# Windowed attention and an ELU layer on one core: the mask instructions of GpSimd placed ahead of two value loads

## The chip, the cores and the metric

The kernel runs on one core of a Trainium2 chip. The metric is the device time of one execution in microseconds (us), of which the median of several runs is taken. The engines are TensorE (PE in the profile; its weight loads are PEld), VectorE (DVE), ScalarE (ACT), GpSimd (POOL) and SyncE (SP). Each has an instruction stream of its own and executes it in order; semaphores tie the streams together. SP, ACT and GpSimd also issue DMA transfers.

## The reference, cut to what matters

The inputs are q, k and v of shape 8 x 8 x 576 x 64 (batch, heads, sequence, head size), and the two weights w_in (512 x 2048) and w_out (2048 x 512), all float32. Attention sees 32 positions to either side; its heads, side by side, are the 4608 x 512 input of a two-layer network with an ELU between the layers:

```python
scores = scale * np.matmul(q, k.transpose(0, 1, 3, 2))
mask = np.abs(pos[:, None] - pos[None, :]) <= 32
scores = np.where(mask, scores, -1000000000.0)
scores = scores - np.max(scores, axis=-1, keepdims=True)
attn = np.exp(scores)
attn = attn / (np.sum(attn, axis=-1, keepdims=True) + 1e-09)
x = np.matmul(attn, v)            # then heads side by side: 4608 x 512
h = x @ w_in
g = np.where(h > 0.0, h, np.exp(np.minimum(h, 0.0)) - 1.0)
out = g @ w_out
```

## The kernel before, in words

Queries are taken in blocks of 64, nine to a batch element, and two blocks make a pair: 36 pairs of 128 tokens. A block looks at 128 keys. For one pair `scores` (line 385) multiplies keys and queries of all eight heads into PSUM, `exponential` (396) takes the exponential on ScalarE into `pu`, `mask` (405) multiplies it on DVE with a band of zeros and ones into `pm`, `pv` (417) multiplies with the values, and `normalize` (426, 429) divides by the sum, which a column of ones in the values gives. Pairs 0 to 3 are treated otherwise: `band` (365) adds a large negative number outside the window to their scores beforehand, from a tile `far`, so that they need no `mask`. The first pair that reads the tile `masks` is pair 4.

The values of a batch element lie in SBUF twice, once from an even block's first key (`V_e`, five pieces) and once shifted by 64 keys (`V_o`, four pieces). For the first element the four pieces of `V_o` are loaded by `load_v_odd` (line 159) and most of `V_e` is copied from them by DVE in `rotate_back` (166). Pair 2 reads `V_o` piece 2 and what was copied from it, pair 3 reads piece 3.

Two pairs make a tile of 256 tokens for the network, 18 tiles in all. A step takes 256 of the 2048 hidden columns: `mm1` multiplies with `w_in` (755), ScalarE takes the exponential (764), DVE or ScalarE subtracts one (775, 773), DVE puts the ELU together (786), and `mm2` multiplies with `w_out` (806). That makes 144 steps; the attention of later pairs is set into them by a table of steps and places, written by hand. Nothing is reordered by a planner: each engine's stream is in the order in which the code calls.

Ahead of the steps stands a front, in straight code. GpSimd, which also converts from float32 to bfloat16 while it loads, issues in this order: `far` and the first fill of `masks` (246 to 257), two pieces of `V_o` with half a piece of `V_e` between them, two pieces `c` of k and q (`load_cast`, 146), the w_in of step 0, the pieces 2 and 3 of `V_o`, the w_in of step 1 in two quarters, the w_in of steps 2 and 3 as one, two parts of w_out (208), the last half piece of `V_e`, two small pieces of q and k, and one more part of w_out. Then come the masks, and after them, from line 547 on, the rest of the weights and the second batch element.

`make_masks` (263 to 278) has five `affine_select` instructions on GpSimd, each of which changes `masks` in place and puts a zero wherever a linear condition on partition and column fails: two on all five 64-column bands (lines 264 and 267), and three on a single band each (271 twice, 275). Beside them, SP and ACT load the first half of q and k at the start, and PE, DVE and ScalarE work through the front of pairs 0 to 3.

Of the kernel before, what the change touches and what calls it, by code (L numbers as in the profile page):

```python
# [21 lines left out]
def kernel(  # L22
# [115 lines left out]
    def load_cast(b, which, part):  # L138
        z, nj = part
        mj = nj if nj < 3 else HJ + 1  # L140
        t = cpool.tile([128, 2, mj * D], BF16, tag=f"c{which}{mj}",
                       name=f"c{which}")[:, :, 0:nj * D]
        qk_c[b, which, z] = t
        src = (q, k)[which][b, :, z:z + NC * nj, :].rearrange(
            "(g h) (c j) d -> c g h (j d)", h=2, j=nj)
        nc.gpsimd.dma_start(out=t, in_=src)
# [10 lines left out]
    def load_v_odd(b, m):  # L157
        lo = 128 * m + WIN
        nc.gpsimd.dma_start(  # L159
            out=V_o[b % 3][:, m, :, 0:D],  # L160
            in_=v[b, :, lo:lo + 128, :].rearrange("h p d -> p h d"))
# [35 lines left out]
    def load_w_in(c, z=0, nz=1):  # L197
        w = D_FF // 4 // nz
        c = c * nz + z
        nc.gpsimd.dma_start(  # L200
            out=w_in_sb[:, :, c * w:(c + 1) * w],
            in_=moe_w_in[:, c * w:(c + 1) * w].rearrange(
                "(o p) f -> p o f", p=128))

    def load_w_out(c, z=0, nz=1):
        n = NFO // 4 // nz
        c = c * nz + z
        nc.gpsimd.dma_start(
            out=w_out_sb[:, c * n:(c + 1) * n, :],
            in_=moe_w_out[c * n * 128:(c + 1) * n * 128, :].rearrange(  # L210
                "(o p) f -> p o f", p=128))
# [51 lines left out]
    def make_masks():  # L263
        nc.gpsimd.affine_select(
            out=masks, in_=masks, compare_op=ALU.is_ge, fill=0.0,
            base=0, pattern=[[0, 5], [-1, QB]], channel_multiplier=1)
        nc.gpsimd.affine_select(
            out=masks, in_=masks, compare_op=ALU.is_ge, fill=0.0,
            base=2 * WIN, pattern=[[0, 5], [1, QB]], channel_multiplier=-1)
        for mi in (0, 4):  # L270
            nc.gpsimd.affine_select(
                out=masks[:, mi, :], in_=masks[:, mi, :],
                compare_op=ALU.is_ge, fill=0.0, base=-WIN,
                pattern=[[0, QB]], channel_multiplier=1)
        nc.gpsimd.affine_select(
            out=masks[:, 3, :], in_=masks[:, 3, :], compare_op=ALU.is_ge,
            fill=0.0, base=128 - WIN - 1, pattern=[[0, QB]],
            channel_multiplier=-1)
# [209 lines left out]
    for which in (1, 0):  # L488
        load_cast(0, which, FRONT_B[which])
    load_w_in(0, 0, 2)  # L490
    for m in (2, 3):
        load_v_odd(0, m)
    for z in (2, 3):
# [5 lines left out]
    for which in range(2):  # L499
        load_cast(0, which, FRONT_C[which])  # L500
    load_w_out(1, 0, 2)
    make_masks()

    idle(10, "y1")
    BOTH = (nc.scalar, nc.vector)
# [401 lines left out]
```

## Time and profile before

| What | Value |
|---|---|
| Median of three runs | 301.42 us (300.98 to 301.87) |
| Profiled execution, its own time | 301.24 us |
| Its span in the profile | 299.5 us |
| PE busy | 294.3 us (98%) |
| DVE busy | 240.7 us (80%) |
| ACT busy | 168.9 us (56%) |
| POOL (GpSimd) busy | 56.4 us (19%) |
| GpSimd's DMA queue (q0) | 45552 packets, 10.03 MB, 43.5% of 16 engines' span |
| The four loads of `V_o`, issue to landing | 4.9 / 6.2 / 7.2 us (least, median, greatest) |
| The five mask instructions | 0.50, 0.47, 0.24, 0.24 and 0.24 us |

Times inside an execution count from the start of the span. The profile is of one execution; what lies around its span (1.74 us) belongs to the time but not to the view. A row of the view in order of time has the start, the duration, the engine, the line, the operation with what it writes and reads, and in brackets the idle time before it with what ended it. Where several instructions of a kind follow one another, one row holds them (x2, x3). A GpSimd row with an operation DMA_DIRECT2D is the issue of a transfer, the writing of its descriptors, and not the transfer itself.

### The profile page before, as it was taken

What the parts mean: (1) busy time and instruction counts of PE and PEld (TensorE: products, weight loads), DVE (VectorE), ACT (ScalarE), POOL (GpSimd) and SP (SyncE); (2) the same over time, 40 slices, a digit from 0 to 9 for tenths busy, and PEclk for the clock granted to TensorE, in tenths of its full rate; (3) what the DMA queues carried; (4) which work ended last, traced back from release to release, by engine and by line L of the source; (5) the groups of instructions that cost most, each with busy time, mean ns of one, the idle gap of its engine ahead of it and who ended that gap; (6) DMA issues with size and microseconds to landing.
All of it is one profiled execution on the core that took longest, in us unless ns stands there. A gap on an engine that the chain in (4) does not pass through costs nothing.

```text
span 299.5 us, 7747 instructions
## 1 busy us (share of the span) xinstructions
PE 294.3 (98%) x3132; PEld 198.7 (66%) x3132; DVE 240.7 (80%) x478; ACT 168.9 (56%) x256; POOL 56.4 (19%) x81
## 2 busy tenths in 40 slices
PE   7999999999999999999999999999999999999996
PEld 3576666676666666666666666666666666666764
DVE  7776787988788888888888789887988787876773
ACT  3883458698655567456745765467535353534342
POOL 8878604520005000410032002300000000000000
PEclk9999999999999999999999999999999999999999
DMA  9999999999968949999899989996921121111012
GB/s 191 173 198 203 189 252 412 355 141 258 205 159 203 239 121 263 231 278 140 161 256 302 192 211 249 311 154 136 272 52 72 35 72 38 70 37 70 2 70 71
DMA packets 94789, 52.74 MB, mean 176 GB/s; under 512 B 78242, under 2 KB 84642, under 8 KB 94754
## 3 DMA queue, kind: packets, MB, share of 16 engines
q1 hardware_dynamic: 47330, 35.68, 44.9%
q0 software_dynamic: 45552, 10.03, 43.5%
q10 hardware_dynamic: 1872, 6.55, 6.3%
q8 instruction: 24, 0.39, 0.6%
q14 instruction: 11, 0.09, 0.1%
HBM read 36.70 MB, written 15.34 MB: 174 GB/s over the span
## 4 chain that ended last, share of the span: by engine, by line
PE 91%; DVE 2%; DMA 2%; POOL 2%; ACT 1%; issue 1%; POOLq 0%; DVEq 0%
PE ps L755 41%; PE psY L806 40%; PE psS L417 4%; PE psS L385 3%; DMA c<-in_q_dram 2%; PE ptx L341 1%; PE psXT L439 1%; DVE m_sb L775 1%; ACT e_sb L764 1%; POOL Vo L159 1%; PE ptx L336 1%; DVE g_sb L786 0%; DVE y_sb L293 0%; ACT pu L396 0%; PE psS L365 0%
## 5 line engine op out<-in xcount | busy, mean ns | idle before, releaser
L764 ACT ACTIVATE e_sb<-ps 128x512 f32<-128x512 f32 (+1 forms) x145 | 86.1, 595 | 112.6 <-PE ps L755 105.7
L755 PE MATMUL ps<-xT,w_in_sb 128*128 128x256 bf16 (+1 forms) x1184 | 149.6, 270 | 0.0
L806 PE MATMUL psY<-w_out_sb,g_sb 128*128 128x512 bf16 (+2 forms) x592 | 147.2, 374 | 0.0
L755 PEld LDWEIGHTS <-w_in_sb 128*128 128x128 bf16 x1184 | 111.0, 98 | 36.6 <-DVE g_sb L786 0.5
L786 DVE SCALAR_TENSOR_TENSOR g_sb<-ps,m_sb 128x512 bf16<-128x512 f32 (+1 forms) x145 | 99.4, 687 | 13.2 <-DVE m_sb L775 0.5
L775 DVE TENSOR_SCALAR m_sb<-e_sb 128x512 bf16<-128x512 f32 (+1 forms) x142 | 61.2, 431 | 33.0 <-ACT e_sb L764 30.8
L806 PEld LDWEIGHTS <-g_sb 128*128 128x128 bf16 x592 | 55.8, 98 | 38.3
L152 POOL DMA_DIRECT2D Ve<-in_v_dram x37 | 32.1, 878 | 128.5 <-PE psS L417 79.5
L396 ACT ACTIVATE pu<-psS 128x1024 bf16<-128x1024 f32 x36 | 36.5, 1021 | 1.4 <-PE psS L385 1.4
L429 DVE TENSOR_TENSOR x_st<-psS,rc 128x512 bf16<-128x512 f32 x36 | 24.9, 692 | 1.2
L291 ACT CAST qkb<-f 128x768 bf16<-128x768 f32 (+2 forms) x29 | 25.1, 864 | 0.6 <-DMA f<-in_q_dram 0.5
L405 DVE TENSOR_TENSOR pm<-pu,masks 128x1024 bf16<-128x1024 bf16 x32 | 21.8, 682 | 0.5 <-ACT pu L396 0.5
L417 PEld LDWEIGHTS <-pm 128*64 128x64 bf16 x512 | 9.6, 110 | 7.3 <-DVE pm L405 6.9
L293 DVE COPY y_sb<-psY 128x512 f32<-128x512 f32 (+1 forms) x18 | 12.2, 676 | 1.4 <-PE psY L806 1.4
L385 PEld LDWEIGHTS <-kT 64*128 64x128 bf16 x560 | 9.4, 95 | 4.7 <-issue 4.0
L291 ACT COPY y_sb<-psY 128x512 f32<-128x512 f32 (+1 forms) x19 | 10.8, 567 | 2.8 <-PE psY L806 2.8
L385 PE MATMUL psS<-qT,kT 64*128 64x64 bf16 x560 | 11.9, 191 | 0.2
L417 PE MATMUL psS<-Ve,pm 128*64 128x65 bf16 x288 | 11.5, 196 | 0.1
L417 PE MATMUL psS<-Vo,pm 128*64 128x65 bf16 x224 | 10.3, 196 | 0.0
L176 DVE COPY Vo<-Ve 64x1040 bf16<-64x1040 bf16 (+2 forms) x22 | 9.1, 414 | 0.7
L291 ACT COPY kT<-ptx 128x512 bf16<-128x512 bf16 (+4 forms) x7 | 6.6, 963 | 2.8 <-PE ptx L336 2.3
L426 DVE RECIPROCAL rc<-psS 128x8 f32<-128x8 f32 x36 | 7.2, 199 | 0.6 <-PE psS L417 0.4
(58 smaller groups left out, 94.4 us busy)
## 6 DMA issues: line engine op xcount, KB each, us to landing
out_dram<-y_sb SPq DMA_DIRECT2D x35, 256.0 KB, 3.8
f<-in_q_dram SPq DMA_DIRECT2D x12, 576.0 KB, 6.9
f<-in_k_dram SPq DMA_DIRECT2D x12, 576.0 KB, 8.7
in_dram<-qkb ACTq DMA_DIRECT2D x10, 576.0 KB, 4.2
Ve<-in_v_dram POOLq DMA_DIRECT2D x21, 128.0 KB, 11.8
w_out_sb<-in_moe_w_out_dram POOLq DMA_DIRECT2D x8, 256.0 KB, 8.9
Ve<-in_v_dram POOLq DMA_DIRECT2D x14, 96.0 KB, 10.8
w_in_sb<-in_moe_w_in_dram POOLq DMA_DIRECT2D x5, 256.0 KB, 7.6
```

The costliest lines, as they stand in the source:

```text
L152: nc.gpsimd.dma_start(out=V_e[b % 3][p0:p1, m, :, 0:D], in_=v[b, :, lo + p0:lo + p1, :].rearrange("h p d -> p h d"))
L291: nc.scalar.copy(d_, s_)
L385: nc.tensor.matmul(psS[:, h % 2, hp * 128 + z * QB:hp * 128 + (z + 1) * QB], lhsT=keys, rhs=qT[b % 2][base:base + 64, hp, QB * qb:QB * (qb ...
L396: nc.scalar.activation(pu, _bap(psS, [psS.ap[0], [1, 1024]]), AX.Exp, scale=SCALE)
L405: nc.vector.tensor_mul(pm, pu, _bap(mm, [mm.ap[0], [0, H], [1, 2 * QB]]))
L417: nc.tensor.matmul(psS[QB * z:QB * (z + 1), par, hp * VD:(hp + 1) * VD], lhsT=pm[:, par * HP + hp, z * QB:(z + 1) * QB], rhs=vv[:, qb // 2 ...
L429: nc.vector.tensor_mul(x_st, _bap(psS, [psS.ap[0], [VD, HP], [512, 2], [1, D]]), _bap(rc, [rc.ap[0], [2, HP], [1, 2], [0, D]]))
L755: nc.tensor.matmul(o, lhsT=w_in_sb[:, do, fo * 128:(fo + 1) * 128], rhs=r, start=(do == 0), stop=(do == NDO - 1))
L764: nc.scalar.activation(e_sb, ps, AX.Exp)
L775: nc.vector.tensor_scalar(m_sb, e_sb, -1.0, None, ALU.add)
L786: nc.vector.scalar_tensor_tensor(g_t[kk][:, z * w:(z + 1) * w, :], ps, 0.0, m_t.pop((kk, z)), ALU.max, ALU.min)
L806: nc.tensor.matmul(sum_of(t, ts, c), lhsT=(g_t[n][:, j, :] if n >= BY_ROWS else g_t[n][:, j, ts * 128:(ts + 1) * 128]), rhs=w_out_sb[:, fi ...
```

## The change

The call of `make_masks` is moved up in the front: past the last part of w_out, two small pieces of q and k, half a piece of `V_e`, two parts of w_out, three loads of w_in and the two value pieces 2 and 3. It now stands right behind the w_in of step 0. No instruction is added, removed or altered, and the streams of the other engines keep their order.

```diff
     for which in (1, 0):
         load_cast(0, which, FRONT_B[which])
     load_w_in(0, 0, 2)
+    make_masks()
     for m in (2, 3):
         load_v_odd(0, m)
     for z in (2, 3):
@@
     for which in range(2):
         load_cast(0, which, FRONT_C[which])
     load_w_out(1, 0, 2)
-    make_masks()
 
     idle(10, "y1")
```

## The prediction

> **What bounds the kernel now.** I read the page's busy shares first: PE is busy for 294.3 us of the 299.5 us span, so a change counts only if it opens or closes a gap on PE. The chain of work that ended last then tells what releases PE in the stretch of the change:
>
> ```profile
> 3.58 0.59 POOL Ve L152
> 4.17 0.88 POOL Vo L159
> 5.05 0.66 POOL c L146
> 5.71 6.18 DMA c<-in_q_dram
> 11.89 0.04 issue
> 11.93 0.58 PE ptx L336 x14
> ```
>
> The reader is to see that GpSimd's issues set the end only up to 5.71 us, and that from 11.93 us on PE carries the chain, to 33.8 us without a break. The masks now run at 16.93 us; they are on no part of it. Next, GpSimd's instructions in order of time (start, duration, engine, line, what, idle time before and its releaser):
>
> ```profile
> 5.71 0.71 POOL L146 DMA_DIRECT2D c<-in_q_dram  x1
> 6.41 0.77 POOL L200 DMA_DIRECT2D w_in_sb<-in_moe_w_in_dram  x1
> 7.16 1.79 POOL L159 DMA_DIRECT2D Vo<-in_v_dram  x2
> 8.90 2.28 POOL L200 DMA_DIRECT2D w_in_sb<-in_moe_w_in_dram  x3
> 11.16 0.72 POOL L208 DMA_DIRECT2D w_out_sb<-in_moe_w_out_dram  x1
> 12.17 0.71 POOL L208 DMA_DIRECT2D w_out_sb<-in_moe_w_out_dram  x1 [0.29 <-DMA c<-in_q_dram]
> 13.49 0.60 POOL L152 DMA_DIRECT2D Ve<-in_v_dram  x1 [0.60 <-DMA w_in_sb<-in_moe_w_in_dram]
> 14.59 0.70 POOL L146 DMA_DIRECT2D c<-in_q_dram  x1 [0.51 <-DMA Vo<-in_v_dram]
> 15.53 0.71 POOL L146 DMA_DIRECT2D c<-in_k_dram  x1 [0.23 <-DMA Vo<-in_v_dram]
> 16.23 0.70 POOL L208 DMA_DIRECT2D w_out_sb<-in_moe_w_out_dram  x1
> 16.93 0.50 POOL L264 TENSOR_SCALAR_AFFINE_SELECT masks<-masks 128x320 bf16<-128x320 bf16 x1
> ...
> 18.61 0.77 POOL L200 DMA_DIRECT2D w_in_sb<-in_moe_w_in_dram  x1
> ```
>
> Counted from the first value load, the 13th issue waits for the 5th transfer (c of q), the 14th for the 6th (w_in), the 15th and 16th for the 7th and 8th (the values of pairs 2 and 3): GpSimd runs at most eight transfers ahead, and in this stretch it is the transfers that hold it up. Last, who needs those values, from DVE's and PE's weight loads in order of time:
>
> ```profile
> 14.33 0.61 DVE L166 COPY Ve<-Vo 64x520 bf16<-64x520 bf16 x2 [0.37 <-DMA Vo<-in_v_dram]
> ...
> 15.26 0.29 DVE L166 COPY Ve<-Vo 64x520 bf16<-64x520 bf16 x1 [0.32 <-DMA Vo<-in_v_dram]
> ```
>
> ```profile
> 15.19 0.20 PEld L417 LDWEIGHTS <-pu 128*64 128x64 bf16 x8 [0.21 <-ACT pu L396]
> ```
>
> Pair 2's values land at about 14.3 us, the copies end at 14.94 us, and PE starts that pair's value products at 15.19 us, having waited for ScalarE. So pair 2's landing has 0.25 us to spare; pair 3's (copy ends 15.55, products at 16.11) has 0.56 us.
>
> **What the Trainium skill says.** "DMA: Bandwidth & Descriptors", section "SWDGE vs HWDGE vs iDMA": GpSimd writes descriptors into rings, which the DMA engines drain; its subsection "Two DMAs through the same engine are not ordered" adds that within one queue of one engine descriptors start in order. So a transfer issued late is late only if its queue has run out of earlier ones. The trace agrees that there is a backlog: the first two value loads, with next to nothing before them on that queue, took 4.9 and 5.2 us from issue to landing, those of pairs 2 and 3 some 7.2. Same page, "Anatomy of one DMA — SWDGE (gpsimd) path": 2.0 us fixed plus bytes at 436 GB/s, an estimate of 2.3 us for the 128 KB here; the trace's 4.9 us beside the first q and k loads is more than twice that, and I use the trace's. "SBUF — State Buffer", section "Who interferes with whom": DVE instructions in a two-port mode and GpSimd block one another for a whole instruction, others with at most one SBUF input do not. The trace fits: DVE's PSUM copy of 128x512 at 18.12 us, under the mask instructions, took 0.42 us, as did the one at 13.54; the SBUF-sourced m_sb at 18.46 took 0.48 against a mean of 0.431.
>
> **The change part by part.** Nothing is added or removed. Five mask instructions (0.50 + 0.47 + two of 0.24 + 0.24) occupy GpSimd from 16.93 to 18.61 us: 1.68 us. They move to 7.16 us, past eleven transfers: two value loads, three of w_in, two of w_out, one of Ve, two of c, one of w_out. All are on GpSimd's queue; SP's queue is passed by nothing.
>
> *The two value loads.* Issues go from 7.16 and 8.03 us to 8.84 and 9.71. What hides this is the backlog. With an empty queue a load would take 4.9 to 5.2 us, so they would land by 14.0 and 14.9 us; the c's and the w_in ahead of them hold them until 14.3 and 15.25 anyway. Cost 0. The margin is 0.3 us in the queue plus 0.25 us on PE: a stall begins only if a value load with nothing before it needs more than 14.56 - 8.84 = 5.7 us. With the backlog gone, the cost would be 1.68 - 0.25 = 1.43 us. I take 0, and keep 0 to 1.43.
>
> *The three w_in loads.* The quarters of step 1 are issued at about 10.6 and 11.3 us; at 5.2 us each they would land by 15.8 and 16.5, and PE first needs them at 16.49 and 17.19. The 512 KB piece goes from some 10.43 to 12.1 us. It took the page's 8.6 us, landing at 19.03, behind the backlog. Empty, I estimate 5.2 us plus 384 KB more at the page's 200 GB/s, 1.9 us: landing at 19.2. Its first product is at about 20.0 us (the 48 products end at 21.77; the last sixteen, of 0.109 us each, are those that need it). Cost 0, at worst what the values cost, not in addition.
>
> *The other six.* The first w_out goes out at 12.84, the second at 13.56 without its 0.29 us wait, Ve at 14.28 without its 0.60. The next two still wait for the values, landing as before, so they go out at about 14.9 and 15.6 against 14.59 and 15.53, and the third w_out at 16.3. Of 1.68 us only about 0.1 is left there: the waits of 0.29 + 0.60 + 0.51 + 0.23 = 1.63 us absorb the rest. Their users come after 21 us. Cost 0.
>
> *What is gained behind.* The w_in load of 18.61 us can be issued at about 17.0. But the queue is full: the page's DMA row stands at 9 through this stretch, and the c issued at 20.85 waits 0.77 us for a w_out to land. An earlier place in a full queue brings no earlier landing. At most, the DMA wait that PE's weight loads show later (0.42 us at 30.36) would go: I take 0 and keep -0.4 to 0.
>
> *DVE and the masks' new neighbours.* Between 7.16 and 8.84 us DVE ends a cast from SBUF at 7.29, then copies from PSUM (0.48 and 0.71 us), which the trace above shows untouched. The cast can lose 0.13 us. The value copies at 8.91 and 14.33 meet descriptor writing in both versions; one blocked copy costs its own 0.29 us. At 8.91 this has 0.7 us before pair 1's products at 11.24; at 14.33 it would eat the 0.25 us. Bound: -0.05 (m_sb at 18.46 freed) to +0.3. I take 0.
>
> *The masks' user* is pair 4's product at 34.97 us, released by ScalarE. Both 8.84 and 18.66 us are far ahead.
>
> Sum against the profiled execution, 301.24 us (span 299.5 and 1.74 around it): 0 + 0 + 0 + 0 + 0, so 301.24 again. The median of the runs shown is 0.18 us above that execution, so 301.4.
>
> **The rivals.**
> *Slower, the values come late.* If issue-to-landing does not shrink, pair 2 lands at 15.99, its copies end at 16.62, and PE stands for 1.43 us at its value products, with score products, w_in products and everything later behind them in PE's order: 302.9 us. It decides from 5.7 us of unqueued latency on. Against it: 4.9 and 5.2 measured, and these beside the first q and k loads. For it: the margin is 0.3 us, and later value loads had 8 us and more to landing, though in a queue.
> *DVE and GpSimd collide at the front.* Up to 0.3 us as bounded above: 301.7 us. For it, one of the first four value copies that already took 0.58 us instead of 0.29. Against it, the front's other work is from PSUM.
> *Faster, the later weights land earlier.* 0.4 us at most by the waits on view, 301.0 us; to pass 0.3% it would need gaps on PE that the trace does not have.
> *The change doesn't do what it says.* GpSimd's program might keep its order; it is written out by hand, so hardly. 301.4 us.
>
> **How the numbers follow.** No effect: 0.60, 301.4, in the spread of the three runs (301.0 to 301.9). Collision: 0.10, 301.7. No real change: 0.02. Values late: 0.20, of which 0.14 near the full 302.9 and the rest between 0.9 and 1.4 us. Faster: 0.08, of which 0.06 beyond 0.3%, by something I don't see. A difference of 0.3% (0.9 us) is about what a measurement of this kernel can tell from none. Chances: faster 0.06, same 0.74, slower 0.20. The range 300.7 to 302.7 leaves out most of the full stall (0.14) and half the unseen gains.
>
> **What would show it.** GpSimd's rows should read masks at about 7.16, values at 8.84 and 9.71, w_in at about 10.6; the idle times before 12.17 and 13.49 should be gone, and Vo's issue-to-landing fall from 7.2 to about 5.5 us. DVE's copies should still start at 14.33 and 15.26, and PE's value products at 15.19 and 16.11. If the copies start after 14.6 and the products follow, the first rival is right and I have mistaken the backlog; if copies of 0.29 turn into 0.58 at 14.33, it is the second.

## The result, and the profile after

The changed kernel took 302.3 us in the median of 22 runs (301.5 to 303.94), the kernel before, run beside it, 301.66 us (300.98 to 303.48). The ratio is 1.0026, with a 95% interval of 1.0014 to 1.0037: slower by some 0.6 to 0.8 us. That is inside the 0.3% that I had called about what a measurement can tell, but 22 runs a side are enough to tell it from no change. I had forecast no change.

GpSimd's instructions in order of time in the changed kernel (start, duration, engine, line, what, idle time before and its releaser):

```profile
6.41 0.77 POOL L200 DMA_DIRECT2D w_in_sb<-in_moe_w_in_dram  x1
7.17 0.51 POOL L264 TENSOR_SCALAR_AFFINE_SELECT masks<-masks 128x320 bf16<-128x320 bf16 x1
...
8.87 1.79 POOL L159 DMA_DIRECT2D Vo<-in_v_dram  x2
10.65 2.24 POOL L200 DMA_DIRECT2D w_in_sb<-in_moe_w_in_dram  x3
12.86 1.44 POOL L208 DMA_DIRECT2D w_out_sb<-in_moe_w_out_dram  x2
14.25 0.65 POOL L152 DMA_DIRECT2D Ve<-in_v_dram  x1
14.89 0.70 POOL L146 DMA_DIRECT2D c<-in_q_dram  x1
16.63 0.71 POOL L146 DMA_DIRECT2D c<-in_k_dram  x1 [1.03 <-DMA Vo<-in_v_dram]
```

Down to 14.89 us this is the timetable of the prediction to within 0.1 us, the two vanished waits included. The last row is not: GpSimd stands 1.03 us for pair 3's values, which I had landing at 15.25 us as before and which landed at 16.35. The chain of work that ended last now runs differently as well:

```profile
10.66 2.20 POOL w_in_sb L200 x3
12.86 9.92 DMA w_out_sb<-in_moe_w_out_dram
22.78 0.04 issue
22.82 1.89 PE psY L806 x8
```

Before, PE carried the chain from 11.93 us on. Now GpSimd's issues carry it to 12.86 us, then a w_out transfer. PE's products with w_in and its first ones with w_out, in the kernel before and then in the changed one:

```profile
18.08 3.69 PE L755 MATMUL ps<-xT,w_in_sb 128*128 128x128 bf16 x48
21.61 1.89 PE L806 MATMUL psY<-w_out_sb,g_sb 128*128 128x512 bf16 x8
```

```profile
18.76 3.70 PE L755 MATMUL ps<-xT,w_in_sb 128*128 128x128 bf16 x48
22.82 1.89 PE L806 MATMUL psY<-w_out_sb,g_sb 128*128 128x512 bf16 x8 [0.37 <-DMA w_out_sb<-in_moe_w_out_dram]
```

PE is 0.68 us late at the first of these rows and 1.21 us late at the second, so w_out itself adds 0.53. Where the 0.68 us come from is seen at PE's weight loads for the value products of pairs 2 and 3:

```profile
15.60 0.34 PEld L417 LDWEIGHTS <-pu 128*64 128x64 bf16 x16 [0.21 <-ACT pu L396]
16.52 0.53 PEld L417 LDWEIGHTS <-pu 128*64 128x64 bf16 x16 [0.21 <-ACT pu L396]
```

Both groups were released by ScalarE after 0.21 us, as before. They start 0.41 us later because PE got the piece `c` of k at 11.23 us instead of 10.83. Within the second group, though, which took 0.34 us before, PE waited for values: its first product starts at 16.72 us, after DVE's copy of them. DVE stands for pair 3's values, and in its order the normalization of pair 2 stands behind that copy. DVE's rows in the kernel before, and then in the changed one:

```profile
16.02 0.69 DVE L429 TENSOR_TENSOR x_st<-psS,rc 128x512 bf16<-128x512 f32 x1
```

```profile
16.37 0.29 DVE L166 COPY Ve<-Vo 64x520 bf16<-64x520 bf16 x1 [1.03 <-DMA Vo<-in_v_dram]
16.94 0.69 DVE L429 TENSOR_TENSOR x_st<-psS,rc 128x512 bf16<-128x512 f32 x1
```

So of the 1.21 us, 0.41 belong to the k piece, 0.27 to pair 3's values and 0.53 to w_out.

What the queue delivered tells more. These are the stretches of the kernel before, and then of the changed one; the last number of a row is the GB/s moved by the DMA engines:

```profile
14.00:16.00 2.00, 2.00 (x42) 1.24 (x40) 1.08 (x4) 1.88 (x2) 1.26 (x3) 1.00 1.63 193
16.00:18.00 2.00, 2.00 (x34) 1.58 (x33) 1.58 (x3) 1.16 (x3) 1.90 (x4) 1.00 1.25 206
18.00:20.00 2.00, 2.00 (x36) 1.91 (x34) 1.84 (x4) 1.54 (x4) 1.96 (x5) 1.00 1.24 203
```

```profile
14.00:16.00 2.00, 2.00 (x55) 1.20 (x50) 1.05 (x3) 1.64 (x2) 1.60 (x3) 1.00 1.60 157
16.00:18.00 2.00, 1.88 (x33) 1.36 (x30) 1.53 (x5) 0.89 (x2) 1.37 (x2) 1.00 1.22 176
18.00:20.00 2.00, 2.00 (x33) 1.69 (x31) 1.48 (x4) 1.72 (x3) 0.81 (x2) 1.00 1.10 173
```

(193 + 206 + 203 - 157 - 176 - 173) GB/s times 2 us is 0.19 MB that did not move, at 200 GB/s about 1 us. It is not made up. SP has a small transfer, the gate, that waits for the last piece of w_in and holds back the loads of the next batch elements; SP's issue of it in the kernel before and in the changed kernel:

```profile
37.12 0.75 SPq L195 DMA_DIRECT2D gate<-w_in_sb  x1
```

```profile
38.91 0.76 SPq L195 DMA_DIRECT2D gate<-w_in_sb  x1
```

The whole series of weights ends 1.8 us later. So there were two suspects: late issue, through the queue, or something that the mask instructions do at their new place, perhaps to the `c` piece of k (the k piece, from here on).

### The profile page after: what moved, and what is told of

Read it like the earlier page. It is cut to its first block, busy times and chain, and to the rows that moved or that the text cites. A ratio compares the mean times of both kernels' runs of the same rounds, so it can differ in the third digit from the quotient of the medians.

```text
span 301.3 us, 7747 instructions
## 1 busy us (share of the span) xinstructions
PE 294.8 (98%) x3132; PEld 198.6 (66%) x3132; DVE 240.8 (80%) x478; ACT 168.9 (56%) x256; POOL 56.6 (19%) x81
## 4 chain that ended last, share of the span: by engine, by line
PE 87%; POOL 4%; DMA 3%; DVE 2%; ACT 1%; issue 1%; POOLq 0%; DVEq 0%
PE psY L806 40%; PE ps L755 39%; PE psS L417 3%; DMA w_out_sb<-in_moe_w_out_dram 3%; PE psS L385 3%; POOL Vo L159 1%; POOL w_in_sb L200 1%; PE ptx L341 1%; DVE m_sb L775 1%; ACT e_sb L764 1%; DVE g_sb L786 1%; POOL c L146 0%; PE psXT L439 0%; DVE y_sb L293 0%; PE ptx L336 0%
```

## The experiments

Theory **late issue**: 1.7 us of delay ahead of the value loads costs, whatever causes it. Rival **mask instructions**: they disturb what runs beside them (the q and k pieces in flight, DVE). Rival **chance**: the late transfers of one profiled execution have little to do with the change. All kernels compute the whole of the reference.

**The same two kernels again.** No edit.

> The kernel before, unchanged, for a second profile of it. All theories: ratio 1.000. If the late landings in the profile of the changed kernel (c of k at 11.2 us, the first w_out at 22.8 us) are chance of one execution, this profile can show such landings too; if they belong to the change, it shows 10.8 and 20.3 us again.

Measured: 0.9999 (0.9991 to 1.0007); k piece at 10.5 us, first w_out product at 21.50, gate at 36.76.

> The changed kernel, unchanged, for a second profile of it. All theories: ratio 1.002 to 1.004. Late issue (the queue loses time because GpSimd writes the value and weight descriptors 1.7 us later): the first product with w_out starts after 22 us again. Chance of one execution: it starts near 21.6 to 22.0 us, and the first profile's 22.8 us was one slow transfer.

Measured: 1.0045 (1.0021 to 1.0069); w_out at 22.61, gate at 38.62, and this time PE waits 0.6 us for a w_in quarter. The late weights come back, though not at one and the same transfer. Chance falls as an explanation of the whole.

**The masks behind the two value loads.**

```diff
     for m in (2, 3):
         load_v_odd(0, m)
+    make_masks()
     for z in (2, 3):
@@
     load_w_out(1, 0, 2)
-    make_masks()
```

> The masks behind the two value loads and ahead of the w_in quarters. Late values (the two value loads are what is hurt): the whole loss goes, ratio 1.000, value copies at 14.3 and 15.3 us. Late issue of the weights (the queue loses time whatever is late): the loss stays, ratio 1.002 to 1.003, the first w_out as late as with the change. Mask instructions disturb the q and k pieces in flight: half or less of it, since they run from 9 us on.

Measured: 0.9994 (0.9979 to 1.001). The w_in quarters go out at 10.81 us, as late as with the change (10.65), and nothing is lost: 201 GB/s from 14 to 20 us, gate at 37.24. That is what the case of late values had said. The weights' own late issue, by this much, costs nothing; the delay has to stand ahead of the value loads.

**Memsets in place of the masks.** The masks stay at their old place.

```diff
     load_w_in(0, 0, 2)
+    hold = cpool.tile([128, 5, QB], BF16, name="hold")
+    for _ in range(5):
+        nc.gpsimd.memset(hold, 1.0)
     for m in (2, 3):
```

> The masks stay at their old place, and five memsets of a scratch tile (about 1.6 us of GpSimd, writing only, more work than before) stand where the change put the masks. Late issue: as slow as the change or slower, ratio 1.002 to 1.004. Mask instructions themselves (they read and write SBUF beside DVE): ratio 1.000 to 1.001, since no mask instruction has moved.

Measured: 1.0046 (1.0032 to 1.0059), values issued at 9.23 us. No mask instruction has moved, and the loss is there.

**An idle wait in place of the masks.** GpSimd's calls from the value loads on are moved, in their order, behind DVE's copies of the first keys, with one small copy ahead of them:

```diff
+    hold = cpool.tile([128, 8], BF16, name="hold")
+    nc.gpsimd.tensor_copy(hold, keys_or_queries(0, 1)[:, 16:24])
     for m in (2, 3):
         load_v_odd(0, m)
```

> The masks stay at their old place. Ahead of the issue of the values of pairs 2 and 3, GpSimd waits until DVE has copied the first keys (8.9 us) and then copies eight columns of them, so that it is idle, not busy, for about 1.7 us. Late issue: as slow as the change, ratio 1.002 to 1.005, first w_out landed after 21.5 us. A busy GpSimd disturbs the q and k pieces in flight (SBUF access beside DVE or the rings): ratio 1.000 to 1.001.

GpSimd's rows of this kernel:

```profile
6.41 0.76 POOL L200 DMA_DIRECT2D w_in_sb<-in_moe_w_in_dram  x1
9.31 0.22 POOL L504 COPY hold<-kT 128x8 bf16<-128x8 bf16 x1 [2.14 <-DVE kT L293]
9.77 1.76 POOL L159 DMA_DIRECT2D Vo<-in_v_dram  x2 [0.24 <-issue]
```

Measured: 1.0074 (1.0054 to 1.0093). GpSimd did nothing for 2.14 us, the values went out 2.6 us late (more than meant), and the loss is larger than the change's. GpSimd executed nothing while it waited, so delay alone is enough for a loss, at 2.6 us.

**Less and more delay.** The same memsets, two and nine.

```diff
-    for _ in range(5):
+    for _ in range(2):      # and 9
```

> As with the five memsets, but two of them: values issued some 0.8 us late instead of 2.05. Late issue with a margin (the backlog hides the first part of the delay): ratio 1.000 to 1.001. Cost in proportion to the delay: two fifths of 1.0046, so about 1.0018.

> Nine memsets: values issued some 3.7 us late, at about 10.9 us. Late issue with a margin of about 1 to 2 us: the values land at about 15.8 us (4.9 us after issue), pair 2's products start near 16.6 instead of 15.2 us and the w_in of step 1 follows late too, 2.4 to 4 us in all, ratio 1.008 to 1.013. If only a disturbance at the start of the weights counts: 1.004 to 1.006, like five memsets.

Measured: 1.0015 (0.9998 to 1.0033) with the values at 8.04 us, too wide to tell either case; 1.0128 (1.0111 to 1.0145) with the values at 11.06 us. With nine, PE waits 0.36 us for pair 3's values, 1.45 for the large piece of w_in and 0.54 for w_out.

**The masks between the two value loads.**

```diff
     for m in (2, 3):
         load_v_odd(0, m)
+        if m == 2:
+            make_masks()
@@
     load_w_out(1, 0, 2)
-    make_masks()
```

> The masks between the two value loads: pair 2's go out at 7.16 us, pair 3's at 9.7 us as with the change. Both value loads matter: a part of the loss, 1.001 to 1.003. Only the queue standing short right behind the w_in of step 0 matters: no loss, 1.000, as with the masks behind both. Pair 3's own landing matters: the whole loss, 1.003, its copy at 15.9 us or later.

Measured: 1.0032 (1.0018 to 1.0046). Pair 2's values go out on time, pair 3's at 10.13 us, 2.1 us late (the masks took longer there, beside DVE's copies). The whole loss: the place right behind the w_in of step 0 is not special. Pair 3's copy ran at 15.96 us, as the case of pair 3's own landing had said, but PE did not wait for it: it got the k piece at 11.51 us and was late itself.

**The change a third time, and the other side of the place.** For the second kernel the first mask instruction, which changes nothing when repeated, stands four times ahead of the values; for the third, the masks and five memsets stand behind the values; for the fourth, the masks stand later than before.

```diff
     load_w_in(0, 0, 2)
+    for _ in range(4):                  # second kernel
+        nc.gpsimd.affine_select(out=masks, in_=masks, ...)
     for m in (2, 3):
         load_v_odd(0, m)
+    make_masks()                        # third kernel
+    for _ in range(5):
+        nc.gpsimd.memset(hold, 1.0)
@@
     load_w_out(1, 0, 2)
-    make_masks()                        # third and fourth kernel
@@
     for which in range(2):
         load_cast(1, which, ONE_A)
+    make_masks()                        # fourth kernel
```

> The changed kernel a third time, for its profile. If the mask instructions slow the k piece in flight: PE starts on it at 11.2 us or later, as in the two profiles of the change so far (11.23, 11.27) and not at 10.4 to 10.95 as in the kernels that have no mask instruction there. Late issue alone: anywhere from 10.4 to 11.3. In both cases the w_in or w_out products of steps 1 to 6 stand for a late weight, and the step that begins at 23.1 us before begins after 23.7.

Measured: 1.0021 (0.9997 to 1.0044); k piece at 11.58 us. That made the k piece late in all four profiles with the masks ahead of a value load, and in none of those without.

> The masks at their old place, and ahead of the values four of their first instruction (which changes nothing when repeated), some 2.2 us of GpSimd that reads and writes SBUF; five memsets of 2.05 us cost 1.0046. Late issue alone: 1.004 to 1.006, PE on the k piece at 10.4 to 10.95 us. Mask instructions slow the k and q pieces too: 1.006 to 1.008, PE on the k piece at 11.2 us or later.

Measured: 1.0038 (1.0025 to 1.0051), values at 9.33 us; k piece at 10.61 us. The loss of late issue is there without a late k piece.

> Values on time at 7.16 us, then the masks and five memsets, so that the w_in quarters and all behind them are issued some 3.7 us late, against 1.9 late with the masks alone behind the values, which cost nothing. If it is the weights' issue that has a margin (about 2 us) and then costs: 1.003 to 1.010, the w_in quarter landed after 16.5 us. If only the value loads' place matters: 1.000 to 1.001.

Measured: 1.0074 (1.0053 to 1.0095). The values are on time, the first w_in quarter goes out at 12.81 us. PE's products with w_in:

```profile
16.51 0.61 PE L758 MATMUL ps<-xT,w_in_sb 128*128 128x256 bf16 x4 [0.20 <-DMA w_in_sb<-in_moe_w_in_dram]
...
22.09 1.21 PE L758 MATMUL ps<-xT,w_in_sb 128*128 128x256 bf16 x8 [2.12 <-DMA w_in_sb<-in_moe_w_in_dram]
```

The quarter costs 0.20 us, the large piece behind it 2.12. So the weights have a margin of their own: 1.9 us late was free, 3.9 us is not.

> The masks later than before, behind the first casts of the second batch element, where GpSimd waits for transfers to land (0.77 and 0.49 us): issues behind the third w_out go out up to 1.7 us earlier than in the kernel before, but into a full queue. Full queue: 1.000. If earlier issue there keeps the queue from losing time: 0.997 to 0.999.

Measured: 1.0005 (0.9992 to 1.0018). Earlier issue of what stands behind the old place gains nothing, as the prediction had it, and no version found beats the kernel before.

**Just short of the change's delay, and the change beside it.** Four memsets; seven of the narrow mask instructions; three of the second wide one. The masks stay at their old place in each.

```diff
     load_w_in(0, 0, 2)
+    for _ in range(4):                  # first kernel
+        nc.gpsimd.memset(hold, 1.0)
+    for mi in (0, 4, 0, 4, 0, 4, 0):    # third kernel
+        nc.gpsimd.affine_select(out=masks[:, mi, :], ...)
+    for _ in range(3):                  # fourth kernel
+        nc.gpsimd.affine_select(out=masks, in_=masks, ...)
     for m in (2, 3):
```

> The masks at their old place, four memsets ahead of the values: issue 1.65 us late, as with the change, by instructions that only write. Late issue alone makes the change's loss: same ratio as the changed kernel beside it within 0.0015, about 1.003, PE on the k piece at 10.4 to 10.95 us. The mask instructions add to it: 1.001 to 1.002, clearly below the changed kernel.

> The changed kernel beside these on one chip: 1.002 to 1.0045, PE on the k piece after 11.2 us if that belongs to the change.

> The masks at their old place, and ahead of the values seven of the narrow mask instructions (one band of 64 columns, 0.24 us each, no effect when repeated): issue some 1.6 to 1.7 us late. Late issue alone: about 1.003, k piece at 10.4 to 10.95 us. The narrow instructions slow the k piece: k piece after 11.2 us, ratio 1.003 to 1.005.

> As before it, with three of the second wide mask instruction (0.54 us with its gap, 1.6 us late). Late issue alone: about 1.003, k piece at 10.4 to 10.95 us. This instruction slows the k piece: after 11.2 us, ratio 1.003 to 1.005.

Measured: 1.0014 (1.0005 to 1.0023), 1.0034 (1.0021 to 1.0047), 0.9996 (0.9983 to 1.0009) and 1.0013 (1.0005 to 1.0021). The k piece came at 10.95, 10.69, 10.79 and 10.59 us: with the change too it can be on time, and the loss is there without it. But memsets of the change's delay should have come within 0.0015 of the change beside them, and are 0.0020 below it: by what was written down, the mask instructions add something. The intervals of the two just overlap. The narrow ones and the second wide one, which late issue alone had put at about 1.003, also cost less.

**The old place filled, and only the wide instructions moved.**

```diff
     load_w_in(0, 0, 2)
+    make_masks()         # first kernel, with the old call kept
+    wide_masks()         # second kernel: lines 264 and 267 here,
     for m in (2, 3):     # lines 271 and 275 at the old place
```

> The masks made at the new place and once more at the old one, where they change nothing: issue of the values as late as with the change (8.87 us), the old place as full as before. Late issue alone: as the change, 1.002 to 1.0045. The emptied old place is part of the loss: 1.000 to 1.0015.

> The two wide mask instructions at the new place (values issued at about 8.25 us, 1.1 us late), the three narrow ones at the old place. Late issue with a margin of about 1.5 us: 0.999 to 1.001. Cost in proportion to the delay: 1.002.

Measured: 1.0026 (1.0004 to 1.0048) and 1.0001 (0.9977 to 1.0024). The emptied old place needs no part in the loss; the two wide instructions alone, 1.0 us of delay, cost nothing that shows, in a wide interval. (In the profile of the second kernel PE stood 0.83 us for pair 3's values all the same: single executions differ.)

All kernels that delay the values, in order of the delay of pair 2's, with the GB/s between 14 and 20 us and the time of the gate in their profiles:

| Delay, us | Ahead of the values | Ratio | GB/s | Gate, us |
|---|---|---|---|---|
| 0 | nothing (kernel before, twice) | 0.9999 | 201, 202 | 37.12, 36.76 |
| 0 (pair 3's 2.10) | masks between the two loads | 1.0032 | 177 | 38.54 |
| 0.88 | two memsets | 1.0015 | 202 | 37.09 |
| 0.99 | two wide mask instructions | 1.0001 | 201 | 37.67 |
| 1.48 | seven narrow | 0.9996 | 195 | 37.58 |
| 1.54 | second wide, three times | 1.0013 | 200 | 37.78 |
| 1.66 | four memsets | 1.0014 | 192 | 38.10 |
| 1.7 | the change, four times | 1.0026, 1.0045, 1.0021, 1.0034 | 168, 193, 200, 171 | 38.91, 38.62, 38.70, 38.32 |
| 1.72 | masks in both places | 1.0026 | 187 | 38.13 |
| 2.07 | five memsets | 1.0046 | 168 | 38.77 |
| 2.17 | first wide, four times | 1.0038 | 175 | 38.30 |
| 2.61 | idle wait | 1.0074 | 179 | 38.30 |
| 3.90 | nine memsets | 1.0128 | 140 | 41.20 |

Up to about 1.5 us little or nothing; beyond it, 1.0128 at 3.9 us is 3.9 us lost for 2.4 us more. The change's 1.7 us lies just past the bend. The rate follows the loss only roughly: in its third profile the change moved 200 GB/s, hardly less than the kernel before, and the gate was late all the same.

The repeat of the change with an undisturbed k piece shows the loss at its cleanest. PE's products with w_out, and later its transposes for the second batch element, with ScalarE's cast that feeds them and SP's gate:

```profile
22.38 1.89 PE L806 MATMUL psY<-w_out_sb,g_sb 128*128 128x512 bf16 x8 [0.76 <-DMA w_out_sb<-in_moe_w_out_dram]
```

```profile
38.32 0.75 SPq L195 DMA_DIRECT2D gate<-w_in_sb  x1
```

```profile
46.48 1.26 ACT L291 CAST qkb<-f 128x1280 bf16<-128x1280 f32 x1 [1.57 <-DMA f<-in_q_dram]
```

```profile
48.28 0.72 PE L341 MATMUL ptx<-ident,qkb 128*128 128x128 bf16 x10 [1.15 <-ACT xT L291]
```

In the kernel before, the first wait is absent (21.61 us above), the cast starts at 44.65 us after 0.47 us of waiting, and the transposes start at 46.44 us without a wait:

```profile
44.65 1.26 ACT L291 CAST qkb<-f 128x1280 bf16<-128x1280 f32 x1 [0.47 <-DMA f<-in_q_dram]
```

```profile
46.44 0.72 PE L341 MATMUL ptx<-ident,qkb 128*128 128x128 bf16 x10
```

0.76 + 1.15 us is 1.91 us, and this profile's span is 301.4 us against 299.5: 1.9 us.

## Why the prediction was wrong

*What bounds the kernel* was read rightly, and so was the timetable of GpSimd's issues down to 14.89 us. *What is gained behind* was right: nothing was, and the masks later still changed nothing. *DVE and the masks' new neighbours*, at nothing, is not refuted: repeated mask instructions cost no more than memsets of like delay. *The masks' user* was never near.

*The two value loads* (cost 0) held in three of the four profiles of the change and failed in the first, where pair 3's values landed 1.1 us late and cost PE some 0.3 us. I had taken 4.9 to 5.2 us as a load's time with nothing before it; with nine memsets, where the queue had run low, the loads took 3.9 to 4.4. But with the change the queue was not empty, and they took 5.7 and 6.6 us in that profile: I had the transfers ahead holding them to the old landings, 14.3 and 15.25 us, and they landed at 14.61 and 16.35. The rival that ended slower had the right cause, but its 1.43 us at pair 2's value products never came; what came at values was pair 3's, once, and most of the loss lay elsewhere.

*The three w_in loads* and *the other six*, both at cost 0, are the steps that failed. I gave each transfer its own budget (issue, latency, first user), assumed that what stands ahead keeps the queue delivering at 200 GB/s, and concluded that a landing moves only if its own budget is spent. Landings moved without that: 201 GB/s between 14 and 20 us fell to 168 and 171 in the worst two profiles of the change. The first w_out, with 8.8 us between its issue (12.84) and its user (21.61) by my timetable, took 9.9 and arrived at 22.8 us. In the second profile PE waited 0.56 us for a w_in quarter. The last w_in, which I had not priced at all because "the queue is full", ended 1.2 to 1.8 us later, and the gate handed that on to the loads of the second batch element. That is the term missing from the sum: in the clean profile (the fourth of the change) 0.76 us at w_out and 1.15 us at the transposes.

The size was bounded rightly: 302.3 us lies in the range of 300.7 to 302.7. That is luck in part: the upper end came from how much of a stall at the values I had left in, and most of the loss was no such stall. I had put the likeliest case at no change, and "slower" at 0.20 by that stall.

How much of the change's loss is late issue stays open. Delay alone costs, as memsets and the idle wait show. But the k piece came 0.40, 0.44 and 0.75 us later than in the first profile of the kernel before in three of the change's four profiles, and PE waited for it. It is issued at 5.02 us in both kernels, ahead of the masks, so late issue is no reason for it. In the third profile that is enough to explain why the first products with w_out start 0.69 us late. Over all 20 profiles it came after 11.2 us in four of the six in which all five masks stand ahead of a value load, and by 10.96 us in the other fourteen. That the mask instructions do this is a rival that no experiment here settles. The loss does not need it (the clean profile, five memsets), but it may add to it, and would fit that 1.66 us of memsets cost 1.0014 and 1.7 us of masks 1.0034 on one chip. A sharp bend would fit that too.

Also open is how the landings fall behind. GpSimd had issued w_in and w_out pieces by 14.3 us that landed as late as 22.8 us, so the queue as a whole was not empty. The page "DMA: Bandwidth & Descriptors" of the Trainium skill, section "Queues, rings and completion order", says that each queue has a ring on each of 16 DMA engines, each with its own tail; that some rings ran short of descriptors while others still had a backlog would fit, and would fit that the first 1.5 us cost little. The views show only a transfer's last landing, but the packed traces hold sixteen for each. In the change's third profile the last piece of w_in had fifteen landings by 37.12 us (36.99 in the kernel before) and its sixteenth at 38.69 (37.10). So a single part does fall behind, and this may be an old lag: the k piece there had its fifteenth landing at 10.30 us and its last at 11.54. Which rings these are, and whether one ran short, the traces do not tell: the shortage is argued, not shown.

## What to carry to other kernels

In this kernel a queue with transfers outstanding was not yet a full one: a delay of issue that was within the budget of each later transfer, taken singly, still made some of them late. So when a step is moved ahead of DMA issues, look not only at the first user of each transfer but at the rate of the queue over the next stretch and at what waits for the last transfer of the series. Delay is easy to test by itself: a few memsets of a scratch tile, or a wait, show how much is free.

## What was not expected of the hardware

With the same transfers in the same order on GpSimd's queue, the rate between 14 and 20 us went with how early they had been issued: 201 to 202 GB/s with up to 1 us of delay ahead of the values, 192 to 200 at 1.5 to 1.7 us of other instructions, 168 to 200 with the change, 140 with 3.9 us. The same 1.9 us of delay placed behind the two value loads left it at 201, and 3.9 us there brought it to 144. A transfer is done with the last of its sixteen landings, and that one can lag alone: by 1.57 us behind the fifteenth at the last w_in of the change's third profile, with 200 GB/s moved as before.
